# Landmark sums of three batches on GpSimd instead of TensorE, with a new order

## The chip, the cores and the metric

The kernel runs on one core of a Trainium2 chip. The metric is the device time of one execution in microseconds (us). Engine names in the profile: PE is the matmul engine TensorE, PEld its weight loads, DVE is VectorE, ACT is ScalarE, POOL is GpSimd, SP is SyncE, which here only issues stores.

## The reference

Inputs q, k, v are 8 batches x 8 heads x 576 tokens x 64 (fp32); w_in is 512 x 2048, w_out 2048 x 512. A Nystrom attention with 32 landmarks a head is followed by a feed-forward layer with a squared ReLU:

```python
q_lm = q.reshape(B, H, 32, 18, D).mean(axis=3)      # landmarks: means of 18 tokens
k_lm = k.reshape(B, H, 32, 18, D).mean(axis=3)
A, Bm, C = sm(q, k_lm), sm(q_lm, k_lm), sm(q_lm, k) # softmax of scaled products
Z = Bm.T / (norm1(Bm) * norminf(Bm) + 1e-06)
for _ in range(6):
    Z = 2 * Z - Z @ Bm @ Z
x = (A @ Z @ C @ v)        # heads side by side: 4608 tokens x 512
h = x @ w_in
out = (relu(h) ** 2) @ w_out
```

## The kernel before

The batches are worked one after the other, in two halves of four heads (r = 0, 1); four heads and 32 landmarks fill the 128 partitions. X[b % 3] holds q (t = 0) and k (t = 1) of a batch in bf16, a partition having the 18 tokens of one landmark of one head, 64 values each. The loads cast fp32 to bf16 and are issued by GpSimd: ldq, ldk, ldv for q, k, v, win and wout for the weights; eight of them may be under way.

For each batch b:

- Landmarks. Batch 0 sums by matmuls against an identity in 64 x 64 blocks (L507) and full ones (L500), batch 1 by L500, batch 2 by L507. Batches 3 to 7 (`ROWS`) load q and k a second time in another layout, XS (lx, L430: two loads of 576 KB in bf16), and sum with 24 matmuls against a 0/1 matrix (lm, L485); lme copies the sums, scaled, from PSUM to LM, and lmt transposes them to LT.
- T (L469): DVE transposes of X, the operand of the score matmuls.
- B: the 32 x 32 softmax (Bmx to Bml), its norm (Bnm to Brn), then six Newton steps: bd (L630) spreads the matrix on a block diagonal, on DVE or GpSimd, N (L693, L698) multiplies, U (L707) updates.
- SS (L729, L724): scores for C and A. C: Cmx (L767), Cex (L770), Cnr (L417) and CT; A: At, Amx, Asb (L1010), Aex, Asu, Arc, Aml (L1020; L965 in batches 0 and 1), Ab.
- CV (L815), Zm (L849), ZC, and W (L886): Z C v times w_in for each head, which stands in for w_in, copied by We to WP.
- F (L1050): first feed-forward matmuls from AT and WP; R (L1071 on ScalarE, L1073 on DVE) takes the ReLU, Q (L1078 on ScalarE, L1080 on DVE or GpSimd) squares it into G.
- O (L1097): second feed-forward matmuls, 36 tiles of 128 tokens, 16 matmuls each; Oe copies out of PSUM, St stores.

Nothing is left to a scheduler at run time. `ORDER` is a list of all operations written out; a word is an operation, `@` gives its PSUM banks, `/A`, `/D`, `/P` its engine. The planner (`Plan.schedule`) goes through the list with a cost for each operation, gives it a planned start, and the instructions are emitted in the order of these starts; each engine then works its own instructions in that order and waits by semaphore for operands. `port` names the engines on which an operation excludes others with the same mark, in the plan alone. `fillers` puts matmuls without use (L1171) into planned gaps of PE until the first O. c0 to c18 build constants; c11 is eight small ScalarE copies into cpick.

Of the kernel before, what the change touches and what calls it, by code (L numbers as in the profile page):

```python
# [54 lines left out]
class Plan:  # L55
# [5 lines left out]
    BLOCK, FETCH, FETCH_LOADED, PROLOG = 256, 3.8, 6.2, 94  # L61
# [36 lines left out]
    def schedule(self, order):  # L98
# [4 lines left out]
        owner, landed, self.history, self.order = [None] * 8, [], [], []  # L103
        for word in order:
# [55 lines left out]
    def fillers(self, until, width, emit):  # L160
# [42 lines left out]
RATE = {"sw": 0.375e6, "hw": 0.2e6, "first": 0.375e6, "then": 0.405e6, "late": 0.29e6}  # L203
T0 = {"PE": 1.1, "ACT": 1.1, "DVE": 1.1, "POOL": 1.31, "SP": 1.1}
# [59 lines left out]
def kernel(  # L264
# [32 lines left out]
    XS = mk("XS", [96, 2, H, 6, D], BF16)  # L297
# [72 lines left out]
    def c_blk(e):  # L370
# [3 lines left out]
        blk2[:], blkb[:, 0:2], blkb[:, 2:4], ALU.add), R=["blkb"], W=["blk2"])  # L374
# [9 lines left out]
    op("c13", {"DVE": 0.1}, lambda e: nc.vector.memset(cmk[:], 0.0), W=["cmk"])  # L384
# [42 lines left out]
    def load_xs(b):  # L427
        for t in range(2):
            src = (q, k)[t][b].rearrange("h (p j) d -> p h (j d)", j=6)
            op(f"lx{b}.{t}", {"POOL": 0.57}, lambda e, t=t, src=src: nc.gpsimd.dma_start(  # L430
                XS[:, t].rearrange("p h j d -> p h (j d)"), src),
# [27 lines left out]
    def attention(b):  # L459
# [17 lines left out]
        def landmarks_rows():  # L477
# [3 lines left out]
            def lmx(e):  # L481
                xs = XS[:].rearrange("p t (r c) j d -> p t r c j d", r=2)
# [7 lines left out]
               lambda e: copy(e, lm[:], view(), scale=LMS), R=[pl_], W=[("LM", i2, r) for r in range(2)])  # L490

# [58 lines left out]
        def sB(e):  # L550
# [20 lines left out]
            bf[:], bl[:], bc(s_[:, 4:6]), ALU.mult), R=[kb("bl"), kb("brc")], W=[kb("bf")], port=("POOL",))  # L571
# [15 lines left out]
        else:  # L587
# [16 lines left out]
            else:  # L604
                op(f"Blo{b}", {"DVE": 0.14, "POOL": p_(64)}, lambda e: eng(e).tensor_tensor(
                    blo[:], bf[:], bb[:], ALU.subtract), R=[kb("bf"), kb("bb")], W=[kb("blo")], port=("POOL",))
# [30 lines left out]
        def bbt(e):  # L637
# [15 lines left out]
           R=[kb("bf"), kb("rn")], W=[(*ks(0), "z")], port=("POOL",))  # L653
# [137 lines left out]
        if dup:  # L791
# [4 lines left out]
               R=[kb("csm"), "cmk"], W=[kb("cmk")])  # L796
# [122 lines left out]
        for u in range(2) if b in TOKENS else ():  # L919
# [28 lines left out]
            for j, (x0, x1) in enumerate(zip(cuts, cuts[1:])):  # L948
# [18 lines left out]
                   R=[*kx_("sa"), *kx_("arc")], W=kx_("An"), port=("POOL",))  # L967
# [219 lines left out]
ROWS = (3, 4, 5, 6, 7)  # L1187
# [23 lines left out]
U0.1 Arc0.0b Asu0.1a Bmx1 N0.2@2 U0.2 Bsb1 CT0.0 Asu0.0a c18 bk1/P ldk2.0 CR0@5 Bex1 CRe0/A N0.3@4
U0.3 N0.4@4 Bsu1 Arc0.0a Brc1 Asu0.1b U0.4 Arc0.1a Bml1 Bmb1/A Aml0.0a win31 ldq2.0 Aml0.0b/P
Blo1/P CV0@0,6 CVe0.0/A win30 ldq2.1 ldk2.1 ldv1.11 N0.5@5 U0.5 Btr1 Zd0@3 Zm0 T1.01 Bcs1@2 BBT1@5
CVe0.1/A ZC0@6 ZCe0 Ap0.0@4 Ab0.0/A SA1.1@6 Bnm1 Bad1 Brn1 Zi1 Yi1 Arc0.1b T1.11 Aml0.1b/P ldv1.10
Aml0.1a/P ldv1.00 W0.0@2 We0.01 We0.00 N1.0@0 W0.1@4 We0.1 T1.10 U1.0 N1.1@1 F0.2@2 R0.2 Amx1.1
U1.1 N1.2@0 U1.2 F0.0@4 R0.0 Asb1.1 Aex1.1 SC1.0@0,2 Cmx1.1 Ap0.1@6 Ab0.1/A N1.3@4 SA1.0@5 Cex1.1
Cmx1.0 Cex1.0 U1.3 F0.4@6 wout0 Q0.0/P Q0.2/P R0.4 Q0.4/P wout1 Asu1.1 N1.4@4 U1.4 F0.6@2 R0.6
N1.5@4 wout2 wout3 Q0.6/P F0.16@0 R0.16 W0.3@6 We0.3 Amx1.0 Crc1 U1.5 Arc1.1 Cmk1 CR1@4 Asb1.0
Aml1.1 F0.22@0 Ap1.1@2 CT1.1 CRe1 CT1.0 Ab1.1 F0.12@4 F0.18@6 R0.18/D Q0.16/A R0.22 Q0.22/A R0.12
Q0.12/P lx3.0 lx3.1 W0.2@2 We0.2/D lm2.0@0 lmc2.00 lmc2.01/D lme2.0 F0.20@4 R0.20 CV1@2,6 CVe1.0  # L1220
F0.26@4 Zd1@0 Aex1.0 Asu1.0 CVe1.1/A Q0.20/A F0.10@2 F0.8@6 Q0.18/A R0.8 R0.10 Q0.8/A Q0.10/P Zm1
ZC1@0 ZCe1.0/D ZCe1.1/D lmt2.0 R0.26/D O0.0@1 O1.0@0 W1.1@2 We1.1 B2@4 Bmx2 Bsb2 Bex2 F0.14@6
# [114 lines left out]
```

## Time and profile before

| what | value |
|---|---|
| median of 3 runs | 264.83 us (264.70 to 265.07) |
| profiled execution | 264.69 us |
| its span, first to last instruction | 263.0 us |
| mean granted PE clock | 0.992 |
| ScalarE busy | 184.8 us (70%) |
| DMA moved | 34.18 MB; HBM read 48.50 MB, written 9.44 MB |

The span leaves out what lies around the instructions, 1.7 us here. A busy time counts an engine from the start to the end of its instructions; matmuls overlap, so the distance from one start to the next says more about PE than a duration does.

### The profile page before, as it was taken

To read this page: it belongs to the slowest core of one execution; us is meant where nothing else is said; L and a number is where in the kernel's file an instruction comes from. 1 tells how busy PE (TensorE), PEld (TensorE's weight loads), DVE (VectorE), ACT (ScalarE), POOL (GpSimd) and SP (SyncE) were. 2 spreads that over 40 slices of the span, in tenths; PEclk is the share of its full clock that TensorE was granted. 3 is DMA by queue.
4 is the path that set the end of the run, shared out by engine and by line. 5 is a ranking of instruction groups with operands and counts; after the bars stand their busy time and mean duration, and the time that the engine had idled before them with its cause. 6 is when DMAs were issued, how large, how long until landed. Compare 5 with 4: busy or idle time off the path is not lost.

```text
span 263.0 us, 7571 instructions
## 1 busy us (share of the span) xinstructions
PE 253.5 (96%) x3098; PEld 141.0 (54%) x3098; DVE 208.8 (79%) x537; ACT 184.8 (70%) x334; POOL 75.5 (29%) x127
## 2 busy tenths in 40 slices
PE   7898999999999999999999999999999999999993
PEld 3465566466454656465545455466454655466542
DVE  2799698887999789997998999988898975657110
ACT  1552698489886799979687469797595896588211
POOL 8458675904303430140315520221010120000000
PEclk9999799999999999999999999999999999999999
DMA  6999999995997399848496399337301214053025
GB/s 105 204 185 205 209 207 205 193 208 113 196 223 151 63 205 212 204 87 176 64 231 107 46 190 227 70 60 139 96 2 40 38 31 101 2 120 81 2 61 140
DMA packets 25123, 34.18 MB, mean 130 GB/s; under 512 B 2432, under 2 KB 14464, under 8 KB 25088
## 3 DMA queue, kind: packets, MB, share of 16 engines
q0 software_dynamic: 19168, 24.25, 56.4%
q1 hardware_dynamic: 5760, 9.31, 13.1%
q8 instruction: 24, 0.39, 0.6%
q10 hardware_dynamic: 160, 0.13, 0.2%
q14 instruction: 11, 0.09, 0.1%
HBM read 48.50 MB, written 9.44 MB: 220 GB/s over the span
## 4 chain that ended last, share of the span: by engine, by line
PE 73%; DVE 15%; ACT 7%; issue 2%; POOL 2%; POOLq 0%; DVEq 0%; ACTq 0%
PE ps L1097 40%; PE ps L1050 19%; ACT RS L1071 3%; PE ps L886 3%; PE ps L815 2%; PE ps L1171 1%; DVE sm L767 1%; PE ps L729 1%; POOL X L424 1%; PE ps L485 1%; DVE G L1080 1%; ACT G L1078 1%; DVE RS L1073 1%; DVE TT L469 1%; DVE WP L415 1%
## 5 line engine op out<-in xcount | busy, mean ns | idle before, releaser
L1097 PE MATMUL ps<-w_out,G 128*128 128x512 bf16 (+1 forms) x592 | 139.1, 374 | 0.0
L1097 PEld LDWEIGHTS <-G 128*128 128x128 bf16 x592 | 54.5, 98 | 53.2 <-issue 5.5
L1050 PE MATMUL ps<-AT,WP 128*128 128x288 bf16 (+2 forms) x512 | 75.3, 286 | 0.9 <-ACT RS L1071 0.4
L1071 ACT ACTIVATE RS<-ps 128x576 bf16<-128x576 f32 (+2 forms) x99 | 62.1, 648 | 11.3 <-PE ps L1050 7.3
L1050 PEld LDWEIGHTS <-WP 128*128 128x128 bf16 x512 | 48.1, 98 | 21.9 <-issue 2.6
L1078 ACT ACTIVATE G<-RS 128x576 bf16<-128x576 bf16 (+2 forms) x80 | 53.6, 688 | 3.3 <-DVE RS L1073 2.4
L411 ACT COPY OS<-ps 128x512 f32<-128x512 f32 (+1 forms) x27 | 15.3, 568 | 18.8 <-PE ps L1097 16.2
L1073 DVE TENSOR_SCALAR RS<-ps 128x576 bf16<-128x576 f32 (+2 forms) x29 | 21.9, 757 | 7.2 <-PE ps L1050 3.5
L630 POOL TENSOR_TENSOR BD<-ST,blkb 128x256 bf16<-128x256 bf16 x15 | 10.5, 700 | 58.7 <-DVE ST L707 53.3
L411 ACT CAST WP<-ps 128x1024 bf16<-128x1024 f32 (+1 forms) x24 | 22.2, 962 | 7.2 <-PE ps L886 7.1
L469 DVE STREAM_TRANSPOSE TT<-X 128x576 uint32<-128x576 uint32 x32 | 24.0, 758 | 0.1
L1080 DVE TENSOR_TENSOR G<-RS 128x576 bf16<-128x576 bf16 (+1 forms) x40 | 18.1, 457 | 5.8 <-ACT RS L1071 5.5
L770 ACT ACTIVATE C<-ps,sm 128x576 bf16<-128x576 f32 x16 | 14.3, 906 | 11.8 <-DVE sm L767 11.8
L707 DVE SCALAR_TENSOR_TENSOR ST<-ST,ps 128x128 bf16<-128x128 bf16 (+1 forms) x48 | 12.8, 266 | 8.0 <-PE ps L693 4.7
L1171 PE MATMUL ps<-onesb 128*128 128x512 bf16 (+1 forms) x42 | 13.1, 404 | 1.5 <-DVE onesb L347 1.5
L440 POOL DMA_DIRECT2D V<-in_v_dram x24 | 13.2, 552 | 3.2 <-DMA XS<-in_k_dram 1.5
L415 DVE CAST WP<-ps 128x1024 bf16<-128x1024 f32 (+1 forms) x10 | 11.7, 1165 | 1.0 <-PE ps L886 0.9
L767 DVE TENSOR_REDUCE sm<-ps 128x1 f32<-128x576 f32 x16 | 11.6, 746 | 0.7 <-PE ps L729 0.5
L415 DVE COPY OS<-ps 128x512 f32<-128x512 f32 x10 | 6.7, 678 | 6.0 <-PE ps L1097 6.0
L630 POOL TENSOR_TENSOR BD<-Bt,blkb 128x256 bf16<-128x256 bf16 x4 | 2.7, 665 | 30.5 <-PE ps L693 17.1
L886 PE MATMUL ps<-w_in,ZC 64*32 64x512 bf16 x256 | 11.2, 397 | 0.1
L1080 POOL TENSOR_TENSOR G<-RS 128x512 bf16<-128x512 bf16 (+1 forms) x8 | 8.9, 1120 | 6.0 <-ACT RS L1071 6.0
(143 smaller groups left out, 304.3 us busy)
## 6 DMA issues: line engine op xcount, KB each, us to landing
out_dram<-OS SPq DMA_DIRECT2D x70, 128.0 KB, 2.5
X<-in_k_dram POOLq DMA_DIRECT2D x16, 288.0 KB, 9.0
X<-in_q_dram POOLq DMA_DIRECT2D x16, 288.0 KB, 7.8
XS<-in_q_dram POOLq DMA_DIRECT2D x5, 576.0 KB, 8.8
XS<-in_k_dram POOLq DMA_DIRECT2D x5, 576.0 KB, 9.9
V<-in_v_dram POOLq DMA_DIRECT2D x8, 288.0 KB, 6.1
w_in<-in_moe_w_in_dram POOLq DMA_DIRECT2D x8, 256.0 KB, 9.9
w_out<-in_moe_w_out_dram POOLq DMA_DIRECT2D x4, 512.0 KB, 9.8
```

The lines of the kernel that those rows point to most:

```text
L411: nc.scalar.copy(o, i)
L415: eng(e).tensor_copy(o, i)
L469: op(f"T{b}.{t}{r}", {"DVE": v_(576)}, lambda e, r=r: nc.vector.transpose(tt[:, t, r].rearrange("p s m e -> p (s m e)").bitcast(U32), x[:, ...
L770: op(f"Cex{b}.{r}", {"ACT": a_(576) + 0.27}, lambda e, r=r: nc.scalar.activation(Cs[r][:].rearrange("p x u -> p u x"), cbanks(r), AF.Exp, ...
L886: nc.tensor.matmul(ps[quad(pos_a(c, r)), pW.at + r, :], lhsT=zcs[r][half, pos_c(c, r), :], rhs=w_in[half, c, 512 * ch:512 * ch + 512], sta ...
L1050: nc.tensor.matmul(ps[:, ph.at + i, 0:w], lhsT=wp[:, r, 128 * ff:128 * ff + 128], rhs=at[:, r, t0:t0 + w], start=(r == 0), stop=(r == 1))
L1071: nc.scalar.activation(rs, pair(ph, w), AF.Relu)
L1073: nc.vector.tensor_scalar(out=rs, in0=pair(ph, w), scalar1=0.0, scalar2=None, op0=ALU.max)
L1078: nc.scalar.activation(g, rs, AF.Square)
L1080: eng(e).tensor_tensor(g, rs, rs, ALU.mult)
L1097: nc.tensor.matmul(bank(po)[:, 0:c1 - c0], lhsT=G[:, f, lo:lo + P], rhs=w_out[:, f, c0:c1], start=(f == 0), stop=(f == NF - 1))
L1171: nc.tensor.matmul(ps[:, j, 0:w], lhsT=onesb[:, 0:P], rhs=x[:, 0:w], start=True, stop=True)
```

## The change

Batches 5, 6 and 7 move from `ROWS` to a new list `SUMS`. For them there are no XS loads and no lm matmuls. GpSimd adds the 18 tokens in X instead: la adds the halves of nine tokens into fp32 (SU, laid over XS, which grows from 96 to 128 partitions), four a batch; lb adds 4 + 4, 2 + 2, 1 + 1 tokens and the ninth, for q and for k. lme then copies from SU in SBUF. The first la of batch 5 waits for the last matmul on XS.

In the plan, GpSimd's adds and further two-operand operations of DVE carry `port`; the price of an instruction fetch for PE, the load rates and `fillers` change, and all of `ORDER` is new.

```diff
-    BLOCK, FETCH, FETCH_LOADED, PROLOG = 256, 3.8, 6.2, 94
+    BLOCK, FETCH, FETCH_LOADED, PROLOG = 256, 3.8, 6.0, 110
...
+                    self.stalls.append((free[e], fetched))
...
-                sw += o.nbytes / RATE["first" if sw < 23.0 else "then" if sw < 48.0 else "late"]
+                sw += o.nbytes / next(r for t, r in RATES if sw < t)
...
+            at = max([at, *(y for x, y in self.stalls if at - 0.1 < x < a)])
...
+RATES = ((12.5, 0.41e6), (23.0, 0.365e6), (48.0, 0.405e6), (85.0, 0.33e6), (1e9, 0.29e6))
...
-    XS = mk("XS", [96, 2, H, 6, D], BF16)
+    XS = mk("XS", [P, 2, H, 6, D], BF16)
+    SU = XS[:].rearrange("p t h j d -> p (t h j d)").bitcast(F32)[:, 0:4 * 9 * D].rearrange(
+        "p (t r s d) -> p t r s d", t=2, r=2, d=D)
...
+        def landmarks_pool():
+            add = lambda e, o, i, y: eng(e).tensor_tensor(o, i, y, ALU.add)
+            flat = lambda a: a.rearrange("p s d -> p (s d)")
+            for t in range(2):
+                ku = [("SU", t, 0), ("SU", t, 1)]
+                for r in range(2):
+                    op(f"la{b}.{t}{r}", {"POOL": p_(576)}, lambda e, t=t, r=r: add(
+                        e, flat(SU[:, t, r]), flat(x[:, t, r, 0:9, :]), flat(x[:, t, r, 9:18, :])),
+                       R=kx(t, r), W=[ku[r], *([("XS", 0), ("XS", 1)] if b == SUMS[0] else ())], port=("POOL",))
+                for i, (n, a, z) in enumerate(((4, 0, 4), (2, 0, 2), (1, 0, 1), (1, 0, 8))):
+                    y = SU[:, t].rearrange("p r s d -> p r (s d)")
+                    sl = lambda v, n=n: slice(D * v, D * (v + n))
+                    op(f"lb{b}.{t}{i}", {"POOL": p_(128 * n)},
+                       lambda e, y=y, sl=sl, z=z: add(e, y[:, :, sl(0)], y[:, :, sl(0)], y[:, :, sl(z)]),
+                       R=ku, W=ku, port=("POOL",))
+            op(f"lme{b}.0", {"ACT": 0.1 + ap_(256), "DVE": v_(256)},
+               lambda e: copy(e, lm[:], SU[:, :, :, 0, :], scale=LMS),
+               R=[("SU", t, r) for t in range(2) for r in range(2)], W=[("LM", i2, r) for r in range(2)])
...
-ROWS = (3, 4, 5, 6, 7)
+ROWS = (3, 4)
+SUMS = (5, 6, 7)
```

`port=("POOL",)` becomes `port=("POOL", "DVE")` for Bml, Blo, Zi and Aml, and c8, c13 and Cmk get `port=("DVE",)`. The start of the two orders, and the place of batch 7's sums in the new one:

```diff
-c0 ldk0.1 c1 ldq0.1 c13 c17 Bce0@0 ldq0.0 ldk0.0 ldq1.0 ldk1.0 c2 c14 c12 c3 lm0.1@6 ldk1.1 c5
-ldq1.1 c15 c6 c11 lmc0.10 lmc0.11 ldv0.10 ldv0.00 win10 ldv0.11 T0.11 c8 T0.01 lme0.1 lmt0.1
...
+c0 ldk0.1 ldq0.1 c1 c17 ldq0.0 ldk0.0 c2 ldq1.0 c5 ldq1.1 ldk1.0 ldk1.1 c3 lm0.1@0 lmc0.10 lmc0.11
+c6 Bce0@3 c9 c13 c10 T0.11 T0.01 lme0.1 lmt0.1 SC0.1@0 c12 c15 T0.00 win01 c18 ldv0.00 win11
+ldv0.11 ldv0.10 ldv1.11 win20 Cmx0.1 Cex0.1 T0.10 T1.00 CT0.1 lm0.0@5 lme0.0 lmt0.0 bk0 B0@0 Bmx0
+Bsb0 Bex0 Bsu0 Brc0 Bml0 Bmb0/A SC0.0@4 Cmx0.0 Cex0.0 c11 Btr0 SA0.1@6 SA0.0@2 Amx0.0a T1.01
...
+Q5.6/A lb7.00 lb7.01 lb7.02 lb7.03 lb7.12 lb7.13 F5.9@6 F5.8@2 R5.8/D F5.10@0 R5.10 R5.9/D O20.3
+Oe20.0/D F5.13@2 Q5.10/A R5.13 Q5.13/A O21.0@0 SS6.0@6,2,4 At6.0 bd6.3/D O21.1 O21.2 N6.3@1
+F5.11@4 Q5.8/A Q5.9/A R5.11 Q5.11/A St16 O21.3 Oe21.0 lme7.0/D Amx6.0 Asb6.0 Aex6.0 U6.3 SS6.1@4
```

By the two orders 36 instead of 29 of the R go to DVE, 4 instead of 8 of the Q to GpSimd, and 16 instead of 15 of the bd to GpSimd.

More of the change, by code (lines that the diff above doesn't have):

```diff
@@ L373 @@
     op("c8", {"DVE": 0.15}, lambda e: nc.vector.tensor_tensor(
-        blk2[:], blkb[:, 0:2], blkb[:, 2:4], ALU.add), R=["blkb"], W=["blk2"])
+        blk2[:], blkb[:, 0:2], blkb[:, 2:4], ALU.add), R=["blkb"], W=["blk2"], port=("DVE",))
     op("c9", {"DVE": 0.3}, lambda e: nc.vector.tensor_copy(
@@ L570, in attention @@
         op(f"Bml{b}", {"DVE": 0.14, "POOL": p_(64)}, lambda e: eng(e).tensor_tensor(
-            bf[:], bl[:], bc(s_[:, 4:6]), ALU.mult), R=[kb("bl"), kb("brc")], W=[kb("bf")], port=("POOL",))
+            bf[:], bl[:], bc(s_[:, 4:6]), ALU.mult), R=[kb("bl"), kb("brc")], W=[kb("bf")], port=("POOL", "DVE"))
         if b in COLS:
@@ L605, in attention @@
                 op(f"Blo{b}", {"DVE": 0.14, "POOL": p_(64)}, lambda e: eng(e).tensor_tensor(
-                    blo[:], bf[:], bb[:], ALU.subtract), R=[kb("bf"), kb("bb")], W=[kb("blo")], port=("POOL",))
+                    blo[:], bf[:], bb[:], ALU.subtract), R=[kb("bf"), kb("bb")], W=[kb("blo")], port=("POOL", "DVE"))
                 def bcl(e):
@@ L652, in attention @@
             st[0][:, :, 1, :], bf[:], bc(s_[:, 10:12]), ALU.mult),
-           R=[kb("bf"), kb("rn")], W=[(*ks(0), "z")], port=("POOL",))
+           R=[kb("bf"), kb("rn")], W=[(*ks(0), "z")], port=("POOL", "DVE"))
         op(f"Yi{b}", {"DVE": 0.14}, lambda e: nc.vector.tensor_tensor(
@@ L795, in attention @@
                 cmx_[:], cmk[:], s_[:, 14:16].unsqueeze(2).unsqueeze(3).to_broadcast([P, 2, 4, 2]), ALU.mult),
-               R=[kb("csm"), "cmk"], W=[kb("cmk")])
+               R=[kb("csm"), "cmk"], W=[kb("cmk")], port=("DVE",))
             pR = Bank(1, "att")
@@ L966, in attention @@
                                            b3(2)[:, at], ALU.mult),
-                   R=[*kx_("sa"), *kx_("arc")], W=kx_("An"), port=("POOL",))
+                   R=[*kx_("sa"), *kx_("arc")], W=kx_("An"), port=("POOL", "DVE"))
             def tr(e, u=u, pT=pT, anv=anv):
@@ L1211 @@
[L1211 to L1222, printed above, removed]
```

186 lines of the change are left out of this document (99 added, 87 removed).

## The prediction

> **What bounds the kernel now.** I read the page's first lines, then the busy times by stage, then what TensorE (PE) waits for once the start is over.
>
> ```profile
> span 263.0 us, 7571 instructions
> PE 253.5 (96%) x3098; PEld 141.0 (54%) x3098; DVE 208.8 (79%) x537; ACT 184.8 (70%) x334; POOL 75.5 (29%) x127
> ```
>
> PE is busy 96% of the span; VectorE (DVE) is next with 79%, GpSimd (POOL) is busy 29%. That a busy PE is also a streaming one has to be seen by stage and by its waits. The columns by stage are the stretch, its length, busy time of PE, PEld, DVE, ACT and POOL, then PE's granted clock, the DMA share and GB/s.
>
> ```profile
> 20.00:30.00 10.00, 9.06 (x205) 5.09 (x204) 8.73 (x32) 3.08 (x9) 8.62 (x14) 0.83 1.22 209
> 85.00:200.00 115.00, 114.56 (x1488) 62.83 (x1486) 103.92 (x271) 90.64 (x160) 27.34 (x47) 1.00 0.68 126
> 200.00:246.00 46.00, 45.83 (x441) 26.53 (x440) 32.44 (x69) 35.50 (x59) 3.19 (x5) 1.00 0.28 60
> ...
> 100.00:115.00 15.00, 14.77 (x218) 8.10 (x217) 14.35 (x43) 13.16 (x22) 2.23 (x5) 1.00 0.75 163
> 145.00:160.00 15.00, 15.00 (x191) 8.01 (x190) 14.52 (x36) 9.13 (x17) 5.16 (x8) 1.00 0.84 130
> ```
>
> The list of PE's waits from 30 us to the end has two rows:
>
> ```profile
> PE ps L1050 <- ACT RS L1071: 0.4, 1, 0.4
> PE ps L1050 <- DVE AT L1023: 0.2, 1, 0.2
> ```
>
> So from 30 us on PE waits 0.6 us in all and streams matmuls otherwise. The time is the start, plus PE's work behind it, plus the drain at the end. Any matmul taken out of the middle shortens the kernel, as long as the operand chains keep up. DVE is the engine that could stop keeping up: between 85 and 200 us it has 115 - 103.9 = 11.1 us idle, in 100 to 115 us only 0.65 and in 145 to 160 us 0.48.
>
> **What the change takes off PE.** The landmark matmuls (L485) of batches 5, 6 and 7, each row followed by what PE starts next:
>
> ```profile
> 101.97 0.84 PE L485 MATMUL ps<-XS,seg 96*32 96x256 bf16 x24
> 102.74 1.04 PE L1097 MATMUL ps<-w_out,G 128*128 128x512 bf16 x4
> ...
> 146.33 0.84 PE L485 MATMUL ps<-XS,seg 96*32 96x256 bf16 x24
> 147.10 0.23 PE L693 MATMUL ps<-ST,BD 128*128 128x64 bf16 x2
> ...
> 167.63 0.84 PE L485 MATMUL ps<-XS,seg 96*32 96x256 bf16 x24
> 168.40 0.63 PE L886 MATMUL ps<-w_in,ZC 64*32 64x512 bf16 x16
> ```
>
> Start to next start is 0.77 us each time. Three of them are 2.3 us, all on PE's path by the waits above: what stands behind each starts that much earlier, and is late by nothing new. The six XS loads (two a batch) leave GpSimd's queue and the DMA engines; PE waits for no DMA after 30 us, so I cost that at nothing.
>
> **What it adds to GpSimd.** Four adds of 576 elements a batch (bf16 in, fp32 out) and two series of 512, 256, 128 and 128 fp32 elements. The nearest two-operand rows of GpSimd, with the XS issue that goes:
>
> ```profile
> L1080 POOL TENSOR_TENSOR G<-RS 128x512 bf16<-128x512 bf16 x7 | 7.7, 1100 | 6.0 <-ACT RS L1071 6.0
> L1080 POOL TENSOR_TENSOR G<-RS 128x640 bf16<-128x640 bf16 x1 | 1.3, 1265 | 0.0
> L965 POOL TENSOR_TENSOR An<-SA,smA 128x320 bf16<-128x320 f32 x2 | 1.5, 739 | 0.0
> L651 POOL TENSOR_TENSOR ST<-Bf,sm 128x64 bf16<-128x64 f32 x5 | 1.5, 294 | 13.1 <-DVE sm L624 13.1
> L430 POOL DMA_DIRECT2D XS<-in_q_dram x5 | 4.1, 815 | 0.0
> ```
>
> From 64 to 512 elements the slope is (1100 - 294) / 448 = 1.8 ns an element; the fp32 row (320 elements, 739 ns) lies on that line (755), so width seems not to matter. An add of 576 is then 1.2 us, and 512, 256, 128, 128 are 1.10 + 0.64 + 0.41 + 0.41 = 2.56 us. A batch is 4 x 1.2 + 2 x 2.56 = 9.9 us, three are 29.8 us in 36 adds (0.83 us each). No row has fp32 results; if they doubled the slope, three batches would be about 49 us. In 85 to 200 us GpSimd is busy 27.3 us, less six issues of 0.82; with 29.8 it would be at 52 of 115 us, with 49 at 71. It has the time either way, so the adds themselves cost PE nothing. Queued behind them on GpSimd are loads of X and V for later batches and some block-diagonal builds (bd). A build behind one add makes its Newton step up to 1.2 us late, which lies inside the ends of the next term; a load late enough to matter would make PE wait for a DMA, which it does nowhere now.
>
> **What it adds to DVE.** No row shows these adds beside DVE, but other pairs show what can happen:
>
> ```profile
> 106.02 0.66 POOL L630 TENSOR_TENSOR BD<-Bt,blkb 128x256 bf16<-128x256 bf16 x1 [10.32 <-PE ps L1050]
> 106.23 0.77 DVE L1080 TENSOR_TENSOR G<-RS 128x576 bf16<-128x576 bf16 x1
> ...
> 48.69 1.42 DVE L965 TENSOR_TENSOR An<-SA,smA 128x512 bf16<-128x512 f32 x1
> 49.55 1.45 POOL L1080 TENSOR_TENSOR G<-RS 128x512 bf16<-128x512 bf16 x1
> ...
> 62.12 1.43 DVE L469 STREAM_TRANSPOSE TT<-X 128x576 uint32<-128x576 uint32 x2
> 62.28 0.66 POOL L630 TENSOR_TENSOR BD<-ST,blkb 128x256 bf16<-128x256 bf16 x1 [9.14 <-DVE ST L707]
> ...
> L1080 DVE TENSOR_TENSOR G<-RS 128x576 bf16<-128x576 bf16 x26 | 11.9, 462 | 0.9 <-ACT RS L1071 0.8
> L630 DVE TENSOR_TENSOR BD<-ST,blkb 128x256 bf16<-128x256 bf16 x15 | 4.3, 285 | 0.3
> L849 DVE TENSOR_TENSOR ZM<-ST,blk 64x128 bf16<-64x128 bf16 x17 | 3.7, 216 | 0.3
> L1020 DVE TENSOR_TENSOR An<-SA,smA 128x640 bf16<-128x640 f32 x4 | 3.6, 908 | 0.1
> L1010 DVE TENSOR_TENSOR SA<-SA,smA 128x640 f32<-128x640 f32 x4 | 3.3, 816 | 0.0
> L417 DVE TENSOR_SCALAR C<-C,sm 128x576 bf16<-128x576 bf16 x7 | 2.5, 360 | 0.1
> ```
>
> At 106 us the squaring (Q) took 0.77 us where its group between 85 and 200 us (the first of the last rows) takes 0.46; it ended 0.32 us after the GpSimd operation did. At 49 us it is GpSimd that waits: 1.45 for its usual 1.10, ending 0.89 us after DVE's multiply. The two transposes at 62 us took 1.43, no more than alone. So two-operand SBUF work excludes itself between the two engines, for at most the length of one instruction, and one-operand work goes on. By the Trainium skill, GPSIMD Engine Reference, section Specifications, the SBUF interface is shared with VectorE instructions that have two SBUF inputs or run in a 2-port mode; for two inputs the trace agrees (0.77 against 0.46 us), for the 2-port mode no run here shows it. That rule speaks against the change: if it takes in the seven one-input scalings of C (L417) too, the blind count below is 81 operations and 9.4 us instead of 74 and 8.6.
>
> If the order were blind to this, GpSimd would be adding for 29.8 / 115 = 26% of that stretch, and DVE has in it about 74 two-operand operations (26 Q, 15 bd, 17 Zm, and four each of the multiply Aml, L1020, and the subtraction Asb, L1010, in two sizes, the larger shown). 19 of them would meet an add and wait about half of one, 0.45 us: 8.6 us of DVE against 11.1 us of idle time. The new plan holds the two apart in its times, and real times will drift from it by less than an add; I take a quarter, 2.2 us, of which the idle time hides most, and let 0.6 us come through to PE. The ends are 0 and 4.3 (half of the blind figure; the tight stretches at 100 and 145 us pass it on).
>
> **The new order at the start.** The first landmark step of batch 0 in the old order:
>
> ```profile
> 6.97 0.70 PE L507 MATMUL ps<-X,ident 64*64 64x128 bf16 x36
> 5.75 1.28 ACT L411 ACT_TABLE_LOAD   x1 [5.75 <-DVE ident L352]
> 7.04 2.02 ACT L411 COPY cpick<-identf 32x64 f32<-32x64 f32 x8
> 9.07 0.55 ACT L413 ACTIVATE LS<-ps 64x128 f32<-64x128 f32 x2
> ...
> 16.76 2.13 PE L500 MATMUL ps<-X,ident 128*128 128x256 bf16 x18
> 18.92 0.24 PE L698 MATMUL ps<-ST 32*32 32x64 bf16 x8
> ...
> 44.63 0.59 PE L1097 MATMUL ps<-w_out,G 128*128 128x512 bf16 x2
> ```
>
> The matmuls end at 7.67, but ScalarE copies their sums (L413) only at 9.07, behind eight copies for cpick (c11). The new order puts c11 far behind, so this step can run up to 1.4 us earlier. Next late are the loads of batch 1: its landmarks (16.76) need all eight X loads, still first in the queue, and the first Newton step (18.92) stands behind them on PE. So I credit 0.6 us, between a gain of 1.4 and a loss of 1.0 (the new order moves two weight loads ahead of the last V loads and rearranges DVE to 30 us). The other moves there (R, Q and copies between ACT and DVE, four squarings fewer on GpSimd) trade pieces of under 1.3 us between engines that are not PE; I cost them at nothing, covered by PE's stream. The end stays: the same last matmuls, copy and stores.
>
> **The sum.** The profiled execution took 264.69 us, 1.7 more than its span. 264.69 - 2.3 - 0.6 + 0.6 = 262.4. The median of the three runs (264.83) is 0.14 above that execution, so the forecast is 262.5 us, its own range 261.0 to 264.0. What a measurement of this kernel can tell from no change is about 0.2%, 0.5 us.
>
> **Rivals.**
> - DVE late by the shared interface, slower. The adds and DVE's 74 operations meet as in the blind count, because the real times drift from the plan; DVE gives up 8.6 of its 11.1 idle us, and in the stretches with half a us to spare the attention chain is late for PE. At 4.3 us on PE: 264.69 - 2.3 - 0.6 + 4.3 + 0.14 = 266.2; without the gain at the start 266.8. It decides once PE loses over 2.9 us in 85 to 246 us. For it speak the 0.77 row and the two tight stretches; against it that the plan holds the two apart, and that GpSimd's present 27.3 us in that stretch cost PE nothing. Chance 0.27.
> - The matmuls go but their time does not come back: batch 7's landmarks now come at the end of a series of eight adds that stands late in GpSimd's queue, its chain is late by as much as PE saves, and PE stands where L485 ran. 264.8 us. For it speaks that the order puts the copy of batch 7's sums (lme7.0) behind batch 6's score matmuls (SS6.0), while its matmuls now run at 167.6 us, well ahead; against it the 0.6 us of waits, which leave that chain slack. Chance 0.08.
> - More than forecast: the start gives its whole 1.4 us and the stretch of low clock goes. A mean clock of 0.83 over 20 to 30 us is 1.7 us of clock lost; with new fillers, which are no longer placed in a planned fetch stall, it may stay full: 264.69 - 2.3 - 1.4 - 1.7 + 0.6 + 0.14 = 260.0. For it speaks that the earlier copies shorten just this latency-bound part; against it that the matmuls there are small in any order, so that low clock can come again elsewhere. Chance 0.10.
>
> **The numbers.** Forecast 0.55, rivals 0.27, 0.08 and 0.10. Faster by over 0.2%: 0.55 + 0.10 = 0.65. Within 0.2%: 0.05 of the second rival and 0.02 of the first, 0.07. Slower: the rest, 0.25 + 0.03 = 0.28. The range from 260.0 to 267.0 takes in the forecast's own and reaches to both outer rivals' centres; it leaves out about half of the largest gain and a third of the collisions, 0.14.
>
> **What the new profile would show.** L485 with 48 matmuls instead of 120, and PE busy some 2 us less; GpSimd near 100 us busy, its adds of 576 at 1.2 us and of 512 at 1.1; the Q group of DVE in the middle still below 0.55 us mean, and PE's waits after 30 us below 2 us in all; ScalarE's L413 of batch 0 near 7.7 us. I am wrong if PE's waits in 85 to 246 us pass 3 us with DVE as releaser (the first rival), if the adds take twice their price, or if the first output matmuls (L1097), at 44.6 us now, begin over a us later than before.

## The result, and the profile after

The changed kernel takes 271.77 us (median of 4 runs, 270.54 to 272.86) against 264.87 of the kernel before (4 runs, 264.70 to 265.07): a ratio of 1.0259, interval 1.021 to 1.0308. It is 6.9 us slower where 2.3 us faster was forecast. The profiled execution took 271.22 us. One thing is needed to read the times: executions of the kernel before come at two levels, near 263.7 us with a mean clock of TensorE of 0.996 or more and near 264.7 us with 0.991 to 0.993, and the trace shown ahead of the prediction is of the upper one, with a clock of 0.83 from 20 to 30 us.

The first lines of the page, the stages (same columns as before), and all rows of over 0.3 us of TensorE's waits from 30 us on:

```profile
span 269.3 us, 7423 instructions
PE 248.6 (92%) x2984; PEld 139.9 (52%) x3025; DVE 214.4 (80%) x530; ACT 187.8 (70%) x342; POOL 100.4 (37%) x156
```

```profile
20.00:30.00 10.00, 8.61 (x215) 5.16 (x210) 9.00 (x35) 4.35 (x13) 8.15 (x14) 1.00 1.20 206
85.00:200.00 115.00, 105.23 (x1266) 58.53 (x1285) 102.89 (x236) 91.79 (x162) 55.65 (x79) 1.00 0.47 90
```

```profile
PE ps L720 <- DVE BD L657: 3.3, 4, 1.5
PE ps L1077 <- ACT C L797: 1.9, 2, 1.4
PE ps L1124 <- issue: 1.9, 12, 0.2
PE ps L720 <- DVE WP L421: 0.7, 1, 0.7
PE ps L889 <- DVE ZM L876: 0.7, 1, 0.7
```

TensorE's busy time between 85 and 200 us fell from 114.6 to 105.2 us. The largest wait is that of the Newton matmul (N, now L720) for bd (now L657), up to 1.5 us at a time; then come F (L1077) behind the exponentials of C (L797), N behind a late copy of WP (L421), and ZC (L889) behind Zm. The copy of WP is itself late: a Q ahead of it on VectorE took 1.46 us beside an addition. The row "L1124 <- issue" (O) is not counted as a loss: 41 matmul records are missing in this trace (2984, against 3025 weight loads), a missing record looks like a pause, and the fastest version below has the same row.

The groups of GpSimd's additions and, between 85 and 200 us, of VectorE's bd, Q (L1107) and Asb (L1037):

```profile
L499 POOL TENSOR_TENSOR XS<-X 128x576 f32<-128x576 bf16 x12 | 15.6, 1301 | 1.1 <-PE ps L491 0.9
L499 POOL TENSOR_TENSOR XS<-XS 128x512 f32<-128x512 f32 x6 | 7.7, 1283 | 0.3
L499 POOL TENSOR_TENSOR XS<-XS 128x128 f32<-128x128 f32 x12 | 5.3, 458 | 0.3
L499 POOL TENSOR_TENSOR XS<-XS 128x256 f32<-128x256 f32 x6 | 4.5, 744 | 0.2
...
L1107 DVE TENSOR_TENSOR G<-RS 128x576 bf16<-128x576 bf16 x17 | 9.9, 590 | 0.7 <-ACT RS L1098 0.6
L657 DVE TENSOR_TENSOR BD<-ST,blkb 128x256 bf16<-128x256 bf16 x11 | 7.9, 719 | 0.2
L1037 DVE TENSOR_TENSOR SA<-SA,smA 128x640 f32<-128x640 f32 x4 | 4.3, 1077 | 0.1
```

A bd takes 0.719 us in the mean where it took 0.285, a Q 0.590 (0.462), the larger Asb 1.077 (0.816). Times their counts that is 4.8 + 2.2 + 1.0 = 8.0 us of VectorE lost; the other groups with two operands kept their times. It comes from few operations: ten are late by 0.1 us or more, by 0.83 us in the mean against the medians of their groups before. How one of them looks on the timeline (start, duration, engine):

```profile
149.91 1.29 POOL L499 TENSOR_TENSOR XS<-X 128x576 f32<-128x576 bf16 x1
...
150.64 2.48 DVE L657 TENSOR_TENSOR BD<-ST,blkb 128x256 bf16<-128x256 bf16 x1
151.14 0.52 POOL L446 DMA_DIRECT2D V<-in_v_dram  x1
151.67 1.28 POOL L499 TENSOR_TENSOR XS<-X 128x576 f32<-128x576 bf16 x1
...
153.04 1.41 DVE L794 TENSOR_REDUCE sm<-ps 128x1 f32<-128x576 f32 x2
...
153.17 0.23 PE L720 MATMUL ps<-ST,BD 128*128 128x64 bf16 x2 [0.92 <-DVE BD L657]
153.81 0.90 ACT L797 ACTIVATE C<-ps,sm 128x576 bf16<-128x576 f32 x1 [2.74 <-DVE sm L794]
...
154.81 0.40 PE L1077 MATMUL ps<-AT,WP 128*128 128x288 bf16 x2 [1.41 <-ACT C L797]
```

The bd begins inside an addition and is through only at 153.12, 0.17 us after the next addition: 2.48 us for an operation of 0.29. TensorE waits 0.92 us for it. The maximum (L794) stands behind it on VectorE, ScalarE's exponential behind that, and TensorE waits another 1.41 us.

### The profile page after: what moved, and what is told of

Its sections match the earlier page's. It is cut to its first block, busy times and chain, and to the rows that moved or that the text cites. A ratio compares the mean times of both kernels' runs of the same rounds, so it can differ in the third digit from the quotient of the medians.

```text
span 269.3 us, 7423 instructions
## 1 busy us (share of the span) xinstructions
PE 248.6 (92%) x2984; PEld 139.9 (52%) x3025; DVE 214.4 (80%) x530; ACT 187.8 (70%) x342; POOL 100.4 (37%) x156
## 3 DMA queue, kind: packets, MB, share of 16 engines
q1 hardware_dynamic: 5760, 9.31, 12.9%
## 4 chain that ended last, share of the span: by engine, by line
PE 72%; DVE 12%; ACT 4%; issue 4%; DMA 4%; POOL 2%; POOLq 0%; DVEq 0%; ACTq 0%
PE ps L1124 39%; PE ps L1077 20%; DMA X<-in_k_dram 4%; PE ps L913 3%; DVE BD L657 2%; PE ps L1198 1%; POOL X L430 1%; PE ps L842 1%; PE ps L756 1%; ACT RS L1098 1%; DVE G L1107 1%; DVE RS L1100 1%; PE ps L720 1%; DVE SA L1030 1%; ACT C L797 1%
## 5 line engine op out<-in xcount | busy, mean ns | idle before, releaser
L1124 PE MATMUL ps<-w_out,G 128*128 128x512 bf16 (+1 forms) x556 | 133.4, 373 | 3.3 <-issue 1.9
L1124 PEld LDWEIGHTS <-G 128*128 128x128 bf16 x592 | 54.5, 98 | 55.0 <-issue 5.5
L1077 PE MATMUL ps<-AT,WP 128*128 128x288 bf16 (+2 forms) x512 | 74.3, 286 | 2.4 <-ACT C L797 1.9
L1098 ACT ACTIVATE RS<-ps 128x576 bf16<-128x576 f32 (+2 forms) x92 | 58.3, 651 | 18.0 <-PE ps L1077 13.3
L1105 ACT ACTIVATE G<-RS 128x576 bf16<-128x576 bf16 (+2 forms) x86 | 57.5, 686 | 4.7 <-DVE RS L1100 3.8
L1077 PEld LDWEIGHTS <-WP 128*128 128x128 bf16 x512 | 48.2, 97 | 22.8 <-issue 4.5
L1100 DVE TENSOR_SCALAR RS<-ps 128x576 bf16<-128x576 f32 (+2 forms) x36 | 26.6, 749 | 14.9 <-PE ps L1077 11.2
L657 POOL TENSOR_TENSOR BD<-ST,blkb 128x256 bf16<-128x256 bf16 x16 | 11.3, 703 | 68.4 <-DVE ST L734 53.6
L797 ACT ACTIVATE C<-ps,sm 128x576 bf16<-128x576 f32 x16 | 14.4, 905 | 10.6 <-DVE sm L794 10.6
L1107 DVE TENSOR_TENSOR G<-RS 128x576 bf16<-128x576 bf16 (+2 forms) x38 | 19.4, 520 | 1.7 <-ACT RS L1098 1.5
L499 POOL TENSOR_TENSOR XS<-XS 128x128 f32<-128x128 f32 (+2 forms) x24 | 17.4, 736 | 0.8
L734 DVE SCALAR_TENSOR_TENSOR ST<-ST,ps 128x128 bf16<-128x128 bf16 (+1 forms) x48 | 12.9, 268 | 5.8 <-PE ps L720 4.4
L499 POOL TENSOR_TENSOR XS<-X 128x576 f32<-128x576 bf16 x12 | 15.6, 1301 | 1.1 <-PE ps L491 0.9
L1198 PE MATMUL ps<-onesb 128*128 128x512 bf16 (+1 forms) x37 | 11.7, 411 | 1.9 <-DVE onesb L353 1.5
L794 DVE TENSOR_REDUCE sm<-ps 128x1 f32<-128x576 f32 x16 | 11.7, 739 | 1.4 <-PE ps L756 1.4
L421 DVE CAST WP<-ps 128x1024 bf16<-128x1024 f32 (+1 forms) x9 | 10.4, 1161 | 2.9 <-PE ps L913 2.9
L720 PEld LDWEIGHTS <-BD 128*128 128x128 bf16 x72 | 6.3, 97 | 12.1 <-DVE BD L657 6.5
L1039 ACT ACTIVATE SA<-SA 128x640 f32<-128x640 f32 (+1 forms) x12 | 8.1, 679 | 5.3 <-DVE SA L1037 5.3
## 6 DMA issues: line engine op xcount, KB each, us to landing
w_out<-in_moe_w_out_dram POOLq DMA_DIRECT2D x4, 512.0 KB, 11.8
```

What stands on the lines that cost most here:

```text
L499: add = lambda e, o, i, y: eng(e).tensor_tensor(o, i, y, ALU.add)
L657: bdiag = lambda e, o, i: eng(e).tensor_tensor(o.rearrange("p r (c m) -> p r c m", c=4), i.unsqueeze(2).to_broadcast([P, 2, 4, M]), blkb[: ...
L797: op(f"Cex{b}.{r}", {"ACT": a_(576) + 0.27}, lambda e, r=r: nc.scalar.activation(Cs[r][:].rearrange("p x u -> p u x"), cbanks(r), AF.Exp, ...
L1077: nc.tensor.matmul(ps[:, ph.at + i, 0:w], lhsT=wp[:, r, 128 * ff:128 * ff + 128], rhs=at[:, r, t0:t0 + w], start=(r == 0), stop=(r == 1))
L1098: nc.scalar.activation(rs, pair(ph, w), AF.Relu)
L1100: nc.vector.tensor_scalar(out=rs, in0=pair(ph, w), scalar1=0.0, scalar2=None, op0=ALU.max)
```

## The experiments

Theory A: an addition of GpSimd with two SBUF operands shuts out VectorE's operations that need the same interface, for longer than the prediction allowed, and the Newton chain hands that on to TensorE. Theory B: the new order is slower whatever the additions do. Theory C: the additions take longer than planned, and what is queued behind them on GpSimd comes late.

**short_adds**

```diff
-  flat(SU[:, t, r]), flat(x[:, t, r, 0:9, :]), flat(x[:, t, r, 9:18, :])
+  SU[:, t, r, 0], x[:, t, r, 0, :], x[:, t, r, 9, :]
-  y[:, :, sl(0)], y[:, :, sl(0)], y[:, :, sl(z)]
+  y[:, :, 0:32], y[:, :, 0:32], y[:, :, 32:64]
```

> The changed kernel, with its order and its instructions, but every GpSimd addition of the landmarks is cut down to 64 elements a lane; most of the sum is left out, so the landmarks of batches 5 to 7 are not the reference's. The 36 additions shrink from about 33 us in all to an estimated 36 x 0.3 = 11 us. Theory A (the additions hold the operand interface, VectorE's two-operand operations wait up to a whole addition, and the Newton chain comes late): most of the 7.7 us of TensorE gaps goes, 262 to 265 us, and the bd group of VectorE falls below 0.32 us in the mean. Theory B (the new order itself is slower, with or without additions): 269 to 271 us. Theory C (the additions are longer than the plan has them, and GpSimd's own queue runs late): also 262 to 265 us; one_operand tells A from C.

Measured: 263.73 us (before, same chip, 264.66; ratio 0.9976, 0.9952 to 1.0000). The additions take 11.9 us. Since the order is the same, both traces can be laid side by side by TensorE's weight loads: from the 900th to the last, 201.73 us pass in the changed kernel and 194.46 here. So 7.3 us of it hang on the length of the additions. bd takes 0.287 us in the mean, as forecast. B falls as the main cause of the loss.

**one_operand**

```diff
-  add = lambda e, o, i, y: eng(e).tensor_tensor(o, i, y, ALU.add)
+  add = lambda e, o, i, y: eng(e).tensor_scalar(out=o, in0=i, scalar1=1.0, scalar2=None, op0=ALU.mult)
```

> The changed kernel with each of the 36 GpSimd additions replaced by an operation with one operand in SBUF (a multiplication by 1.0) over the same number of elements, at the same place of the same queue; the second summand is left out, so the landmarks of batches 5 to 7 are not the reference's. Theory A (the second SBUF operand shuts VectorE out): VectorE's bd, Q and Asb stay at their free times of about 0.29, 0.45 and 0.81 us beside these operations, and the time falls to 262 to 265 us. Theory C (GpSimd is occupied, so its loads, its products and the landmarks come late): 269 to 271 us, as long as these operations last as long as the additions did (1.3 us for 576 elements). Theory B (the order alone): 269 to 271 us too.

Measured: 266.32 us, ratio 1.0073 (1.0043 to 1.0103). Groups of GpSimd and of VectorE's bd, 85 to 200 us:

```profile
L499 POOL TENSOR_SCALAR XS<-X 128x576 f32<-128x576 bf16 x12 | 20.3, 1694 | 1.0 <-PE ps L491 0.9
L499 POOL TENSOR_SCALAR XS<-XS 128x512 f32<-128x512 f32 x6 | 8.9, 1491 | 0.3
...
L657 DVE TENSOR_TENSOR BD<-ST,blkb 128x256 bf16<-128x256 bf16 x11 | 4.4, 404 | 0.2
```

GpSimd is occupied longer than by the additions (40.8 us in all against 33.3), and yet 5.4 of the 8.0 us between short_adds and the changed kernel are gone (4.9 of 7.5 by the ratios). That speaks against C. The expected 0.29 us of bd is missed: 0.404, and 266.32 lies 1.3 us above A's range. One-operand work of GpSimd still holds VectorE, but for less than 0.5 us at a time (the longest bd took 0.75 us).

**split_adds**

```diff
+  c = 192 if o.shape[-1] == 576 else 64
+  for k in range(0, o.shape[-1], c):
+      eng(e).tensor_tensor(tt(o), tt(i), tt(y), ALU.add)      # tt: columns k to k + c
```

> The changed kernel with every GpSimd addition cut into pieces, the same sum: three of 192 elements for each of 576, and pieces of 128 for the others, 84 additions instead of 36. By the changed kernel's rows (128 elements 0.457 us, 256 0.73, 512 1.27) they take about 43 us in all instead of 33. Theory A with VectorE let in between two instructions of GpSimd: a wait is at most about 0.6 us instead of 1.3, the longest bd falls from 2.48 us to below 1 us, and the time to 265 to 269 us. Theory A with GpSimd keeping the interface over a row of back-to-back additions: no gain or a loss, 271 to 276 us. Theory C (GpSimd's queue late): 10 us more of GpSimd work, 272 to 275 us.

Measured: 268.15 us, ratio 1.0142 (1.0118 to 1.0167); the additions take 43.4 us. 10 us more of GpSimd work and 3.6 us less time: again against C, and inside A's first range. The longest bd is 0.97 us, but one Q took 1.52, over two pieces and a DMA issue behind them: it waited some 1.1 us, where 0.6 at most was expected.

**short_56**: the diff of short_adds for `b in (5, 6)`.

> The changed kernel with the additions cut down to 64 elements in batches 5 and 6 alone; those of batch 7 are whole. Most of the sum of batches 5 and 6 is left out, so their landmarks are not the reference's. It divides the loss: in the progress of the feed-forward matmuls the changed kernel loses about 5 us against the kernel before between 115 and 200 us and about 2 us behind 200 us. Theory A: 263 to 266 us, within 1 us of short_adds if the later loss is only the earlier one handed on, and 2 to 3 us above it if batch 7's additions cost time of their own. Theory B: 269 to 271 us. Theory C: as theory A.

Measured: 266.80 us, ratio 1.0094 (1.0064 to 1.0123). That is 0.8 us above A's range. Batch 7's additions cost 3.1 us by themselves (2.8 by the weight loads); the trace has the pattern of 150.64 us above again, a bd of 2.19 us. From 63 to 145 us its weight loads keep their distance from those of short_adds within 0.02 us. The loss of batch 7 is made at its own additions and is not handed on from the batches before.

**beside**: a measurement outside the kernel.

```diff
+  for other, n in ((g_none, 0), (g_add_f32, 30), (g_add_bf, 30), (g_one, 16), (g_dma, 8)):
+      for _ in range(n):
+          other()                                    # GpSimd
+      for one in (d_two_bf, d_copy_bf, d_two_bf, d_scalar_bf, d_two_f32, ...):
+          one()                                      # VectorE
```

> Not the kernel but a measurement by itself (it computes nothing of the reference and writes constants): VectorE runs the same 24 operations five times, alone and beside a row of back-to-back GpSimd operations: additions of 512 fp32 elements, additions of 576 bf16 elements into fp32, one-operand multiplications of 576 elements, and issues of DMAs. VectorE's operations are products and differences with two SBUF operands (256 bf16, 640 fp32), one with an SBUF and a PSUM operand, and copies, a transpose and a reduction with one operand. Theory A: beside the additions each run of two-operand operations with SBUF operands waits for the end of an addition, some 0.6 us in the mean and 1.3 at most, or longer where GpSimd is let in first; beside one-operand operations the wait is below 0.5 us; those with one SBUF operand and those with a PSUM operand keep their times alone within 0.05 us. If copies of bf16 (VectorE's fast form) share the interface too, they wait like the two-operand ones. Beside DMA issues alone: no wait by theory A, up to 0.6 us if the descriptors' writing holds the interface.

VectorE alone, then beside additions of 512 fp32 elements, then beside one-operand operations (which starts at 123.70 us):

```profile
26.93 0.23 DVE L113 COPY DO<-DA 128x256 bf16<-128x256 bf16 x1
27.19 0.29 DVE L103 TENSOR_TENSOR DO<-DA,DB 128x256 bf16<-128x256 bf16 x1
...
28.51 0.29 DVE L116 COPY DP<-DF 128x256 f32<-128x256 f32 x1
29.58 0.81 DVE L128 TENSOR_REDUCE DM<-DF 128x32 f32<-128x640 f32 x1
30.31 0.28 DVE L109 SCALAR_TENSOR_TENSOR DO<-DA,ps 128x128 bf16<-128x128 bf16 x1
30.51 0.44 DVE L125 STREAM_TRANSPOSE DP<-DF 128x256 f32<-128x256 f32 x1
```

```profile
39.09 1.17 DVE L113 COPY DO<-DA 128x256 bf16<-128x256 bf16 x1
40.29 1.37 DVE L103 TENSOR_TENSOR DO<-DA,DB 128x256 bf16<-128x256 bf16 x1
...
43.70 1.24 DVE L116 COPY DP<-DF 128x256 f32<-128x256 f32 x1
...
46.73 0.81 DVE L128 TENSOR_REDUCE DM<-DF 128x32 f32<-128x640 f32 x1
47.46 0.27 DVE L109 SCALAR_TENSOR_TENSOR DO<-DA,ps 128x128 bf16<-128x128 bf16 x1
47.66 0.43 DVE L125 STREAM_TRANSPOSE DP<-DF 128x256 f32<-128x256 f32 x1
...
126.21 0.64 DVE L116 COPY DP<-DF 128x256 f32<-128x256 f32 x1
```

Beside an addition a bf16 copy takes 1.17 us for 0.23, the product of two 1.37 for 0.29, an fp32 copy 1.24 for 0.29. The reduction, the operation with a PSUM operand and the transpose keep their times. So the shut-out takes in copies with one operand, which theory A had expected to go on. The Trainium skill, SBUF — State Buffer, section Who interferes with whom, has it so: copies from SBUF to SBUF may take the pair of ports shared with GpSimd, reductions never do, and whoever comes first keeps it for its whole instruction; beside additions these rows agree. Beside one-operand GpSimd operations of 1.65 us they differ: the fp32 copy is held 0.35 us, not the rest of the instruction.

**bd_copies**

```diff
+  for c in range(4) if e == "DVE" else ():
+      eng(e).tensor_copy(o[quad(c), :, quad(c)], i[quad(c)])
```

> The changed kernel with VectorE's 20 block-diagonal products of the Newton steps of batches 2 to 7 (bd, two SBUF operands, 0.29 us free) made by four copies each of a 32x64 block (one operand), onto tiles whose other blocks are set to zero once; GpSimd's own bd stay products; the result is the same. Theory A: the bd waits (4.8 us of VectorE's 9.0 us of excess, and the gaps of 0.66, 1.47, 0.25, 0.91 and part of 1.41 us before TensorE's N step that VectorE's bd ended) go, at an estimated cost of 20 x 0.1 us of VectorE: 267 to 269 us. If copies of bf16 are shut out by the additions as well: 271 to 273 us. Theory C (GpSimd's queue late): 271 to 273 us.

Measured: 282.37 us, ratio 1.0672 (1.0626 to 1.0717), 9.4 us above even the worst expectation. Both halves of theory A's expectation were wrong. Copies are shut out too (one took 2.01 us), as beside shows. And four of them cost far more than 0.1 us over the product:

```profile
L663 DVE COPY BD<-Bt 32x64 bf16<-32x64 bf16 x8 | 1.4, 172 | 0.1
```

0.172 us each, free, is 0.69 for four, in every one of 20 links of the Newton chain: an estimated 20 x 0.40 = 8.0 us more than the products, of the 10.6 us by which this run is above the changed kernel.

**short_lm**: short_adds with the 24 matmuls put back ahead of lme in batches 5 to 7, on tiles that are there anyway.

> short_adds (the changed kernel with its additions cut down to 64 elements) with 24 matmuls of 96x256 put back on TensorE for each of batches 5 to 7, as many and of the size of those that the change removes, ahead of the copy of the landmarks; they read tiles that are loaded anyway and nobody reads their sums, so nothing else waits for them, and no second load is made. It prices the one gain of the change by itself. If TensorE is the bound there, as the prediction's first term has it, 3 x 0.77 = 2.3 us come back: 265.5 to 266.5 us against 263.73. If TensorE has slack of its own at these three places, less: 263.7 to 264.7 us, and then the gain of the change was never 2.3 us.

Measured: 265.73 us, ratio 1.0068 (1.0046 to 1.0091). It is 2.0 us above short_adds by the medians and (1.0068 - 0.9976) x 264 = 2.4 by the ratios: the removed matmuls are worth what the first term of the prediction gave them. Against the kernel before it is 1.8 us slower by the ratio: with as many matmuls as before, the new order and the additions cut to a third cost 1.8 us together. So B holds as a second, smaller cause, of 1.8 us at most; what the short additions have of it was not measured.

**ordered_adds**

```diff
+            if o.eng == "DVE" and "DVE" in o.port:
+                held = made[-1].name
+            elif o.name[:2] in ("la", "lb"):
+                tc.add_manual_dep(made[-1], held, ...)     # the addition waits for it
```

> The changed kernel with one thing added: each addition waits for the VectorE operation with two SBUF operands that the plan has ahead of it (a semaphore, no new operation), so an addition can no longer slip in ahead of a bd, Q or Asb that is late by the plan. Theory A in its full form (the plan excludes the two engines from each other, but on the chip both drift, and the addition that starts a moment before a Newton step's bd holds it): the worst waits (bd 1.36, 1.45 and 2.48 us) go, GpSimd comes later instead, 266 to 269 us. If the waits only move to GpSimd's queue, whose bd and loads then come late: 270 to 273 us.

> ordered_adds once more, in more rounds, because it is the one version so far that may be ahead of the kernel before (0.998, interval 0.9961 to 0.9999). Theory A: the additions cost TensorE nothing once they are kept in the planned order, and what is left is the matmuls' 2.0 us (short_lm) less what the new order costs beside them: 262.8 to 263.4 us against 263.7, a ratio of 0.996 to 0.999. If the first measurement was luck: a ratio of 1.0 or more.

Measured: 263.17 us (before 263.73; ratio 0.9980, 0.9961 to 0.9999), and in the second measurement 263.36 (before 263.92; ratio 0.9979, 0.9963 to 0.9996). That is almost 3 us better than theory A's range, over 8 us ahead of the changed kernel, and 0.2% ahead of the kernel before. The additions are whole and as long as ever, 32.7 us. The loss of the changed kernel is gone beyond doubt; the gain over the kernel before is at the edge of what these runs can tell, for only one of the 22 executions here was at the upper level and 11 of 36 of the kernel before, and without these it is 0.3 us in the mean. What the second trace has in place of the rows above (TensorE's waits of 0.3 us and more from 30 us on, bd and Q from 85 to 200 us):

```profile
PE ps L1124 <- issue: 1.9, 12, 0.2
PE ps L751 <- DVE RS L1100: 0.3, 1, 0.3
PE ps L1077 <- ACT C L797: 0.3, 1, 0.3
```

```profile
L1107 DVE TENSOR_TENSOR G<-RS 128x576 bf16<-128x576 bf16 x17 | 8.1, 483 | 0.7 <-ACT RS L1098 0.6
L657 DVE TENSOR_TENSOR BD<-ST,blkb 128x256 bf16<-128x256 bf16 x11 | 3.6, 332 | 0.2
```

The waits for bd are gone. This settles A against C: the same additions in the same queue cost TensorE nothing once they keep the place that the plan gave them. It also shows what the drift was. In the plan, batch 6's second addition stands behind the Asb of batch 4, and here it waits for it. First this trace, then the changed kernel:

```profile
121.97 0.82 DVE L1037 TENSOR_TENSOR SA<-SA,smA 128x640 f32<-128x640 f32 x1
122.89 1.27 POOL L499 TENSOR_TENSOR XS<-X 128x576 f32<-128x576 bf16 x1 [1.61 <-DVE SA L1037]
```

```profile
120.84 1.29 POOL L499 TENSOR_TENSOR XS<-X 128x576 f32<-128x576 bf16 x1
120.85 1.45 DVE L657 TENSOR_TENSOR BD<-ST,blkb 128x256 bf16<-128x256 bf16 x1
...
125.87 1.87 DVE L1037 TENSOR_TENSOR SA<-SA,smA 128x640 f32<-128x640 f32 x1
```

In the changed kernel the addition began at 120.84 us, 5 us ahead of that Asb: GpSimd, with nothing to wait for, ran ahead of the plan and put the addition in front of a bd at 120.85.

**ordered_pieces**: split_adds and ordered_adds together.

> Both remedies at once: the additions cut into pieces of 192 and 128 elements (84 of them, as in split_adds), each waiting for the VectorE operation with two SBUF operands ahead of it in the plan. Theory A: a VectorE operation finds at most one piece, about 0.55 us, in its way: 264 to 267 us, better than split_adds (268.15) and ordered_adds alone. If GpSimd's own lateness decides, worse than split_adds: 269 us or more. It would have to be below 264 us to beat the kernel before.

Measured: 263.88 us, ratio 1.0004 (0.9988 to 1.0020). 4.3 us better than split_adds, but 0.7 behind whole additions in order: with the order kept, cutting only adds 10 us of GpSimd work.

**ordered_bd**: the wait at la5.00, la6.01, lb6.11, la7.01 and la7.10 alone.

> The changed kernel with the wait of ordered_adds at five of the 36 additions alone: those with a Newton step's bd ahead of them in the plan (one of batch 5, two of batch 6, two of batch 7). It tells what part of the loss comes over the Newton chain. By the changed kernel's gaps on TensorE, 3.3 us end with a bd and 1.4 us with the exponentials queued behind a held bd, together 4.7 of 7.3 us; the others stand behind held Q and Asb (0.70 before L889, 0.53 before L1077, 0.74 before L720). Theory A with the Newton chain as the main place: 266 to 268 us. If those five waits put the whole row of additions behind them into its planned place: 263 to 264.5 us, as ordered_adds. If the Newton chain is not the place: 270 us or more.

Measured: 270.18 us, ratio 1.0229 (1.0202 to 1.0256), a miss: 1.6 us gained where 4 to 6 were expected (1.4 us by the weight loads from the 900th on; the intervals of the two ratios overlap). The time alone would fall to the third reading, that the Newton chain is not the place. The trace says otherwise: no gap of TensorE ends with a bd any more, so the 3.3 us and the 1.4 behind them did go. But a new one came:

```profile
121.72 1.27 POOL L499 TENSOR_TENSOR XS<-X 128x576 f32<-128x576 bf16 x1 [3.41 <-DVE BD L657]
...
123.54 1.30 POOL L499 TENSOR_TENSOR XS<-X 128x576 f32<-128x576 bf16 x1
...
124.21 4.38 DVE L1037 TENSOR_TENSOR SA<-SA,smA 128x640 f32<-128x640 f32 x1
...
124.78 0.68 POOL L657 TENSOR_TENSOR BD<-ST,blkb 128x256 bf16<-128x256 bf16 x1
125.40 1.27 POOL L499 TENSOR_TENSOR XS<-XS 128x512 f32<-128x512 f32 x1
...
126.62 1.27 POOL L499 TENSOR_TENSOR XS<-X 128x576 f32<-128x576 bf16 x1
...
129.00 0.58 PE L581 MATMUL ps<-LT 32*32 32x32 bf16 x16 [2.63 <-DVE SA L1030]
```

The addition at 123.54 has no wait, although the plan has it behind this very Asb. It starts 0.67 us ahead of it, and Asb is held over four back-to-back GpSimd operations, 4.38 us for 0.82. One step out of place is enough; waiting at some places moves the collision to the next.

**before_again**

> The kernel before, once more, for a trace of its start in another execution: its runs come at two levels, near 263.7 and near 264.7 us, and the one profiled so far granted TensorE 0.66 of its clock from 25 to 30 us. 263.6 to 265.0 us. If the trace shows no such slice, its first output matmul should start about 1 us ahead of the 44.63 us of the first trace, and the start of the changed kernel (43.48 us) then gained nothing; if it shows the slice again, this stays open.

Measured: 263.69 us, the lower level. Its stage of 20 to 30 us has a clock of 1.00, and the first weight load of O is here:

```profile
L1097 PEld LDWEIGHTS <-G x592: 94/98/100, 43.6 to 257.5; 128*128 128x128 bf16 x198
```

It starts at 43.6 us, in the changed kernel at 43.5, with 674 weight loads ahead of it here and 685 there.

All in one table. The gaps are the sum of stretches of over 0.15 us, from 42 us on, in which TensorE runs neither a matmul nor a weight load, worked out from each trace:

| kernel | median us | additions us | gaps us |
|---|---|---|---|
| bd_copies | 282.37 | 33.0 | 12.9 |
| changed | 271.77 | 33.3 | 7.3 |
| ordered_bd | 270.18 | 33.0 | 5.4 |
| split_adds | 268.15 | 43.4 | 4.8 |
| short_56 | 266.80 | 19.0 | 3.7 |
| one_operand | 266.32 | 40.8 | 3.2 |
| short_lm | 265.73 | 11.8 | 0.9 |
| ordered_pieces | 263.88 | 42.4 | 1.3 |
| short_adds | 263.73 | 11.9 | 1.2 |
| ordered_adds | 263.17 | 32.7 | 0.8 |
| before_again | 263.69 | none | 0.2 |

The time follows the gaps, not the length of the additions; short_lm and before_again stand apart because they have 72 matmuls more.

## Why the prediction was wrong

- **The matmuls, -2.3 us.** Right: 48 of 120 are left, and the three groups are worth 2.0 to 2.4 us (short_lm).
- **The additions, 9.9 us a batch and nothing on TensorE.** Sized 12% low: the additions with fp32 results lie above the line of the other rows, 1.30 us for 576 elements instead of 1.2 and 1.28 for 512 instead of 1.10, 33.3 us in all instead of 29.8, nowhere near twice. That their time on GpSimd costs TensorE nothing is right (ordered_adds, 32.7 us).
- **VectorE's collisions, 2.2 us of which 0.6 reach TensorE.** This is the step that failed. The blind count was 8.6 us, and 8.0 came; that the two agree is partly luck, for the count had 19 meetings of 0.45 us and there were ten waits of 0.83. The quarter rested on the sentence that real times drift from the plan by less than an addition. On an engine that is idle half of the time (busy 55.7 of 115 us) nothing bounded the drift: an addition ran 5 us ahead of the operation that it stands behind in the plan. The second support, that a wait lasts "at most the length of one instruction", fell as well: 2.48 us over two additions, 4.38 over four operations. The third, that VectorE's idle time hides most of it, took VectorE's idle share of a stretch for slack. The operations that were hit are links of a chain, N waits for bd and bd for U, and there idle time elsewhere hides nothing. Of the 7.3 us of gaps only 3.4 lie in the two tight stretches, 100 to 115 and 145 to 160 us. 7.3 us on TensorE stand against the 8.0 on VectorE, well past the upper end of 4.3.
- **The start, -0.6 us.** Read against one trace of the upper level. Against the lower one the first O begins 0.1 us earlier (43.5 and 43.6), with 11 more weight loads done. The copy of batch 0's sums begins at 8.4 us in the changed kernel, not at 7.7.
- **The other moves of the new order, nothing.** Mis-sized: up to 1.8 us by short_lm. They arise behind the start: from the first weight load of O to the end of the span short_lm takes 220.3 us and before_again 218.4. Gaps are 0.7 us of it (0.9 against 0.2); where the rest arises was not found.
- **The rivals.** The first had the mechanism and the sign, and its mark of over 3 us of waits with VectorE as releaser came. Its 266.2 us is 5.6 us short, for the three reasons above. Batch 7 late in GpSimd's queue is not what happened: its additions cost 3.1 us, by the same collisions. The clock of the third stayed full in two of the changed kernel's four executions and not in the others (0.993 and 0.994); in the kernel before it is worth about 1 us, the distance of the two levels, not 1.7.

In sum, from the lower level: 263.7 - 2.2 (matmuls) + 1.8 (order) + 7.3 (length of the additions) = 270.6. The median of 271.77 lies between executions of both kinds: those with a full clock took 270.54 and 271.22, the others 272.32 and 272.86. Like with like it is 270.6 against 270.9, and 0.3 us are not accounted for.

## What to carry to other kernels

Work that is put on an idle engine must be tied to the place the plan gives it, if it shares anything with a busy one: here one semaphore wait for each addition, on the operation that the plan has ahead of it, turned a loss of 2.6% into a time level with the kernel before or 0.2% ahead of it, and waits at five of 36 places gave back only 1.6 of 8 us. A collision is priced by the chain that it hits, not by the busy share of the engine. Before a term is set to a quarter of a bound, look for what enforces the quarter; a mark that exists in a plan alone enforces nothing.

## What the runs showed of the hardware

- An operation of VectorE that is shut out by GpSimd can stay so over several instructions: 4.38 us over additions and a bd that follow each other without a pause. Where the additions stand 0.08 us apart (beside), VectorE gets in after each; whether the pause decides was not tried.
- It goes the other way too: an addition that meets a running difference of 640 fp32 elements takes 1.86 us instead of 1.26 (beside).
- Copies from SBUF to SBUF with one operand, bf16 or fp32, are shut out like products (1.17 to 1.24 us for 0.23 and 0.29); transposes, reductions and operations with a PSUM operand are not.
- In the 2.48 us case 0.47 us lie between the two additions, filled by a DMA issue, and VectorE did not get in; nor did the Q of 1.52 us in split_adds during such an issue. Yet a bd of the changed kernel at 87.93 us ended 0.15 us after its addition, with an issue running, and beside DMA issues alone VectorE lost 0.05 us at most. What tells these cases apart was not tried.
